# Two pooled PSUM buffers in place of one four-bank tile, in a fused long-convolution and gated feed-forward kernel

## The chip, the cores and the metric

The kernel runs on one core of a Trainium2 chip. The metric is the device time of one execution in microseconds, the median of several runs. Profiles are of one execution each, taken by the hardware profiler; their times count from the start of the span.

## What is computed

The input `x` (2048 tokens, 640 channels, bf16) is layer-normalised; a gated convolution and a gated feed-forward block of the normalised input are added to it:

```python
x = A_q
xn = _layernorm(x, axis=-1)
# A: k_shift = causal 4-tap filter of k, per channel;  kv = k_shift * v
#    y = irfft(rfft(kv, padded to 2S) * rfft(ssm_k, padded to 2S))[:S] + kv * ssm_D
#    result: xn * y
# B: (sigmoid(xn @ w_gate) * (xn @ w_up)) @ w_down      (640 -> 1728 -> 640)
return x + A(xn, k, v, ...) + B(xn, ...)
```

## The kernel before

Two streams of work share the engines. The **feed-forward** goes over four token tiles of 512 tokens. For each tile TensorE (PE) does 13 `gate` steps (L225) and 13 `up` steps (L233) of five 128x512 matmuls, one `both` step (L240) for the last half block, and 16 `down` steps (L252) of seven 128x320 matmuls, two to an output. ScalarE (ACT) applies the sigmoid (L231), VectorE (DVE) multiplies (L238) and adds the projection into `x` (L262). Four transposes `xn_tr` (L211) prepare the next tile. Their PSUM buffers come from a pool of four one-bank buffers, `psG`.

The **convolution** goes over five chunks of 128 channels. A transform of 2048 points is done as two matmul stages forward and two back, with trips through DRAM to rearrange the data between them. The steps of a chunk:

- `kv_op` (L289): the 4-tap filter times `v`, on DVE, in 16 operations; `h_tr` (L281), twice: eight PE transposes of the filter, then an ACT copy into `kvh` (L287).
- `st1` (L317), eight times: four 128x256 matmuls (L328), an ACT copy of 128x1024 to `t1` (L331). Each second one is written to DRAM (`wr1`).
- `rd2` reads it back rearranged, `st2` (L349), four times: sixteen 32x32 matmuls of 512 columns (L355) into all four banks, an ACT copy of 128x2048 (L357).
- `prod` (L362), a shuffle (L366) and a product (L368) on DVE.
- `inv1` (L371), twice: 64 small matmuls into all four banks (L383), an ACT copy of 128x2048 (L386); then `wr2` to DRAM and `rdb` back (one buffer `bi`).
- `inv2` (L402), twice: sixteen matmuls (L409); DVE multiplies by `xn` straight out of PSUM (L413) and adds into `x` (L414).

All of these use one PSUM tile, `pc`, four banks of 512 fp32 columns (L269). `st1`, `h_tr` and `inv2` take half of it by `two` (L272), which flips between banks 0-1 and banks 2-3; `st2` and `inv1`, the middle stages, use the whole. With `psG` this fills the eight banks.

The waits between engines are derived by the framework from which tiles an instruction touches; a pool hands out a buffer again when all users of the tile that last held it are done.

The order of all instructions is written by a planner inside the kernel (L449 on). It keeps estimates of when each engine is free and when each piece of data is ready, and takes in turn a step of the feed-forward sequence or, where its inputs and buffers would be ready, a step of the convolution's chains. For each step a list gives engine, duration, needs and products; `C` (L485) counts halves of `pc`, so that a step needs the half of two uses before, and a middle stage takes two. The planner's order fixes each engine's queue; SP's queue of DMA issues too.

Of the kernel before, what the change touches and what calls it, by code (L numbers as in the profile page):

```python
# [10 lines left out]
BF16 = mybir.dt.bfloat16  # L11
F32 = mybir.dt.float32
U16 = mybir.dt.uint16
ACT = mybir.ActivationFunctionType
ALU = mybir.AluOpType
# [4 lines left out]
P = 128  # L20
# [3 lines left out]
NQ = 4  # L24
# [33 lines left out]
def kernel(  # L58
# [14 lines left out]
    nc = tc.nc  # L73
# [14 lines left out]
    res = ctx.enter_context(tc.tile_pool(name="res", bufs=1))  # L88
    cv = ctx.enter_context(tc.tile_pool(name="cv", bufs=1))
    dr = ctx.enter_context(tc.tile_pool(name="dr", bufs=1, space=bass.MemoryType.DRAM))  # L90
    psC = ctx.enter_context(tc.tile_pool(name="psC", bufs=1, space=bass.MemoryType.PSUM))
    psG = ctx.enter_context(tc.tile_pool(name="psG", bufs=4, space=bass.MemoryType.PSUM))

    ident = res.tile([P, P], BF16, name="ident")
# [8 lines left out]
    SM = SMt.bitcast(BF16)  # L103

    x = res.tile([P, NB, DM], BF16, name="x")
    xn = res.tile([P, NB, DM], BF16, name="xn")
# [158 lines left out]
        sync.dma_start(outr[:, b, :], x[:, b, :])  # L265

    pc = psC.tile([P, 4, 512], F32, name="pc")  # L269
    turn = [0]  # L270

    def two(dtype):  # L272
        turn[0] ^= 1
        t = pc[:, 2 * turn[0]:2 * turn[0] + 2, :]
        return t if dtype == F32 else t.bitcast(dtype)

    def add_D(c):
        d = cin[c]
        nc.gpsimd.tensor_tensor(d["hn"][:, 0:1], d["hn"][:, 0:1], d["dcl"][:, :], ALU.add)

    def h_tr(c, part):  # L281
        d = cin[c]
        hv = d["hn"].rearrange("c (p b) -> c b p", b=NB)
        pt = two(BF16)[:, 0, :].rearrange("p (i c) -> p i c", i=8)
        for i in range(8):
            nc.tensor.transpose(pt[:, i, :], hv[:, 8 * part + i, :], ident[:])  # L286
        nc.scalar.copy(out=d["kvh"][:, 8 * part:8 * part + 8, 1, :], in_=pt)  # L287

    def kv_op(c, n):  # L289

# [23 lines left out]
    def quad(i):  # L314
        return slice(32 * i, 32 * i + 32)

    def st1(c, n):  # L317

        h, n4 = divmod(n, 4)
        d = chunks[c]  # L320
        if n == 0:
            d["d1"] = dr.tile([P, 2, NB, 2 * P], BF16, name="d1", bufs=2)
        if n % 2 == 0:
            d["t1"] = cv.tile([P, 8, 2, P], BF16, name="t1", bufs=2)
        ps = two(F32).rearrange("p k (i f) -> p (k i) f", i=2)
        for i in range(4):
            b = 4 * n4 + i
            nc.tensor.matmul(ps[:, i, :], lhsT=S1[:, b, h, :], rhs=cin[c]["kvh"][:, b, :, :],  # L328
                             start=True, stop=True)
        o = 4 * (n % 2)  # L330
        nc.scalar.copy(out=d["t1"][:, o:o + 4, :, :].rearrange("p b s c -> p b (s c)"), in_=ps)  # L331
        d[n // 2] = d["t1"]

    def wr1(c, k):
# [14 lines left out]
    def st2(s):  # L349

        d = groups[s]
        d["xz"] = cv.tile([P, 3, 8, P], BF16, name="xz", bufs=3)
        for g in range(4):
            for q in range(NQ):
                nc.tensor.matmul(pc[quad(g), q, :], lhsT=SM[quad(q), 0, :],  # L355
                                 rhs=d["t2"][quad(q), 2 * g:2 * g + 2, :], start=True, stop=True)
        nc.scalar.copy(out=d["xz"][:, 0:2, :, :].rearrange("p s (q e) c -> p q e s c", q=NQ),  # L357
                       in_=pc.rearrange("p q (e s c) -> p q e s c", e=2, s=2))

    swap = [(i + 16) % 32 for i in range(32)]  # L360

# [9 lines left out]
    def inv1(y):  # L371

        c, y2 = divmod(y, 2)
        d = chunks[c]
        if y2 == 0:
            d["d2"] = dr.tile([32, P, P], BF16, name="d2", bufs=2)
        ao = cv.tile([P, 16, P], BF16, name="ao")
        for o in range(2):
            xz = groups[2 * y + o]["xz"]
            for i in range(2):  # L380
                for q in range(NQ):
                    for g in range(4):
                        nc.tensor.matmul(pc[quad(q), g, 256 * o:256 * o + 256], lhsT=SM[quad(g), 1 + i, :],  # L383
                                         rhs=xz[quad(g), 1 + i, 2 * q:2 * q + 2, :],
                                         start=(i == 0), stop=(i == 1))
        nc.scalar.copy(out=ao.rearrange("p (s g e) c -> p g s (e c)", s=2, g=4),  # L386
                       in_=pc.rearrange("p g (s f) -> p g s f", s=2))
        d["ao"] = ao

    def wr2(y):  # L390
# [11 lines left out]
    def inv2(c, n):  # L402

        cs = slice(c * P, (c + 1) * P)
        ps = two(F32).rearrange("p k (i c) -> p (k i) c", c=P)
        for i in range(8):
            b = 8 * n + i
            for h in range(2):
                nc.tensor.matmul(ps[:, i, :], lhsT=TB[:, h, b, :], rhs=chunks[c]["bi"][:, h, i, :],  # L409
                                 start=(h == 0), stop=(h == 1))  # L410
        bs = slice(8 * n, 8 * n + 8)
        yx = cv.tile([P, 8, P], BF16, name="yx", tag="tmp")
        nc.vector.tensor_tensor(yx[:, :, :], ps, xn[:, bs, cs], ALU.mult)  # L413
        nc.vector.tensor_tensor(x[:, bs, cs], x[:, bs, cs], yx[:, :, :], ALU.add)  # L414


# [23 lines left out]
    xn_tr(0, 3, "dve")  # L440
    add_D(0)
    h_tr(0, 0)
    h_tr(0, 1)


# [39 lines left out]
    def C(i=0, back=2):  # L485
        k = count["C"] + i
        return ("C", k), (("C", k - back) if k >= back else None)
# [5 lines left out]
    def prior(tag, *k):  # L493
        return (tag,) + k if min(k) >= 0 else None

    def s_st1(c, n):
        def ops():
            mk, nd = C()
            n4 = n % 4
            k = 4 * c + n // 2  # L500
            o = [("PE", 0.45, [nd, "S1", ("kv", c, n4 // 2), ("h", c, n4 // 2)], [("st1", c, n)]),
                 ("ACT", 0.92, [("st1", c, n), prior("d1", k - 2)], [mk, ("t1", c, n)])]
            return o
        return st1, (c, n), ops
# [8 lines left out]
    def s_st2(s):  # L513
        def ops():
            m0, n0 = C()
            m1, n1 = C(1)
            return [("PE", 0.47, [n0, n1, ("t2", s), "SM"], [("st2", s)]),
                    ("ACT", 1.65, [("st2", s), prior("inv1", (s - 3) // 2) if s > 2 else None], [m0, m1, ("xh", s)])]
        return st2, (s,), ops

    def s_prod(s, n):
# [2 lines left out]
    def s_inv1(y):  # L524
        def ops():
            m0, n0 = C()
            m1, n1 = C(1)
            return [("PE", 0.75, [n0, n1, ("prod", 2 * y + 1)], [("inv1", y)]),
                    ("ACT", 1.65, [("inv1", y), prior("d2", y - 1)], [m0, m1, ("ao", y)])]
        return inv1, (y,), ops  # L530

    def s_rdb(c, n):
# [3 lines left out]
    def s_inv2(c, n):  # L536
        def ops():
            mk, nd = C()
            return [("PE", 0.95, [nd, ("bi", c, n), ("xn", 2 * n + 1, 3), "TB"], [("inv2", c, n)]),
                    ("DVE", 1.15, [("inv2", c, n)], [mk, ("yx", c, n)]),  # L540
                    ("DVE", 0.62, [("yx", c, n)], [("xa", c, n)])]
        return inv2, (c, n), ops

    def s_htr(c, part):
        def ops():
            mk, nd = C()
            return [("PE", 0.55, [nd, ("D", c), ("va", c)], [("htr", c, part)]),
                    ("ACT", 0.92, [("htr", c, part), prior("st1", c - 2, 7)], [mk, ("h", c, part)])]
        return h_tr, (c, part), ops
# [217 lines left out]
```

## Time and profile before

| | us |
|---|---|
| median of 3 runs | 287.39 (286.69 to 287.74) |
| the profiled execution | 286.87 |
| its span, first to last instruction | 285.1 |
| PE busy | 240.5 (84%) |
| DVE busy | 181.2 (64%) |
| ACT busy | 151.0 (53%) |
| POOL busy | 29.1 (10%) |
| DMA, share of 16 engines' time, queue 1 | 64.2% |

The PE figure counts matmuls with modelled ends; neighbouring matmuls overlap, so start-to-start distances tell more than lengths. The mean granted TensorE clock was 0.999. By time of start, the four token tiles' feed-forward parts begin at about 15, 76, 152 and 228 us; the first `st1` starts at 26.26, the last `inv2` at 273.56.

### The profile page before, as it was taken

How to read it: one execution, taken by the hardware profiler on the slowest of the kernel's cores; microseconds unless marked ns; L12 is line 12 of the kernel's file. 1: busy time of each engine (PE TensorE's matmuls, PEld its weight loads, DVE VectorE, ACT ScalarE, POOL GpSimd, SP SyncE). 2: the span in 40 equal slices, each digit the busy share in tenths (PEclk: the TensorE clock that was granted, in tenths of full speed). 3: DMA queues.
4: the chain of work that ended last, by engine and by line, in shares of the span. 5: the costliest groups of instructions: out<-in, count | busy, mean ns of one | idle time of the engine just before them, and what ended most of it. 6: DMA issues, size and time to landing. Idle time of an engine off the chain costs nothing. (4 is left out here: it accounts for less than half of the span.)

```text
span 285.1 us, 5834 instructions
## 1 busy us (share of the span) xinstructions
PE 240.5 (84%) x2428; PEld 138.4 (49%) x2428; DVE 181.2 (64%) x312; ACT 151.0 (53%) x156; POOL 29.1 (10%) x40
## 2 busy tenths in 40 slices
PE   0498988998888888897888788888878999999994
PEld 0444444566544433465564344443556644544773
DVE  3539959498788969889675455241564647683461
ACT  2733365146777667643677555666623977445000
POOL 4300108110010338010000000000000000000000
PEclk9999999999999999999999999999999999999999
DMA  6999798988878786861967430564642547502274
GB/s 198 246 356 368 186 302 247 264 202 200 256 243 236 199 242 232 258 228 39 245 180 240 155 143 2 181 190 148 222 149 76 183 111 226 147 2 77 74 281 163
DMA packets 84310, 54.84 MB, mean 192 GB/s; under 512 B 46844, under 2 KB 77372, under 8 KB 84028
## 3 DMA queue, kind: packets, MB, share of 16 engines
q1 hardware_dynamic: 83996, 53.95, 64.2%
q10 hardware_dynamic: 288, 0.52, 0.6%
q8 instruction: 19, 0.31, 0.5%
q14 instruction: 7, 0.06, 0.1%
HBM read 36.12 MB, written 18.35 MB: 191 GB/s over the span
## 5 line engine op out<-in xcount | busy, mean ns | idle before, releaser
L238 DVE TENSOR_TENSOR hT<-sig,pu 128x512 bf16<-128x512 bf16 x52 | 35.6, 684 | 57.9 <-PE pu L236 46.4
L228 PE MATMUL pg<-xnT,w 128*128 128x512 bf16 x260 | 65.8, 385 | 0.0
L259 PE MATMUL pd<-wd,hT 128*128 128x320 bf16 x448 | 65.4, 300 | 0.0
L236 PE MATMUL pu<-xnT,w 128*128 128x512 bf16 x260 | 65.2, 382 | 0.0
L331 ACT CAST t<-pc 128x1024 bf16<-128x1024 f32 x40 | 40.5, 1011 | 33.4 <-PE pc L328 27.6
L231 ACT ACTIVATE sig<-pg 128x512 bf16<-128x512 f32 x52 | 31.1, 598 | 38.9 <-PE pg L228 37.1
L259 PEld LDWEIGHTS <-hT 128*128 128x128 bf16 x448 | 42.6, 98 | 17.3 <-issue 1.4
L328 PE MATMUL pc<-kvh,S1t 128*128 128x256 bf16 x160 | 23.9, 272 | 26.0 <-ACT t L331 14.9
L357 ACT CAST xz<-pc 128x2048 bf16<-128x2048 f32 x20 | 37.3, 1863 | 14.3 <-PE pc L355 14.2
L228 PEld LDWEIGHTS <-w 128*128 128x128 bf16 x260 | 24.9, 99 | 28.4 <-issue 2.2
L236 PEld LDWEIGHTS <-w 128*128 128x128 bf16 x260 | 24.4, 98 | 28.2 <-issue 2.7
L328 PEld LDWEIGHTS <-S1t 128*128 128x128 bf16 x160 | 15.4, 97 | 35.1 <-issue 30.1
L262 DVE TENSOR_TENSOR x<-pd,x 128x320 bf16<-128x320 f32 x32 | 15.6, 488 | 23.1 <-PE pd L259 23.0
L368 DVE TENSOR_TENSOR xz<-xz 128x2048 bf16<-128x2048 bf16 x20 | 24.6, 1232 | 0.6
L307 DVE TENSOR_TENSOR acc<-acc,tmp 128x1024 bf16<-128x1024 bf16 x30 | 22.5, 748 | 1.0
L386 ACT CAST ao<-pc 128x2048 bf16<-128x2048 f32 x10 | 18.7, 1865 | 5.0 <-PE pc L383 4.9
L305 DVE TENSOR_TENSOR tmp<-kx,sc 128x1024 bf16<-128x1024 bf16 x30 | 20.6, 688 | 0.2
L187 DVE BATCH_NORM_STATS2 st<-x 128x6 f32<-128x320 bf16 x32 | 13.9, 475 | 4.6 <-DMA x<-in_A_q_dram 4.6
L287 ACT COPY kvh<-pc 128x1024 bf16<-128x1024 bf16 x10 | 10.1, 1013 | 10.7 <-PE pc L286 10.6
L215 PE MATMUL pt<-ident,xn 128*128 128x128 bf16 x80 | 7.7, 242 | 9.6 <-ACT xn L204 9.6
L413 DVE TENSOR_TENSOR yx<-pc,xn 128x1024 bf16<-128x1024 f32 x10 | 12.2, 1218 | 5.0 <-PE pc L409 5.0
L366 DVE STREAM_SHUFFLE xz<-xz 128x512 f32<-128x512 f32 x20 | 14.4, 722 | 0.0
(40 smaller groups left out, 149.9 us busy)
## 6 DMA issues: line engine op xcount, KB each, us to landing
d<-t SPq DMA_DIRECT2D x20, 512.0 KB, 3.1
t<-d SPq DMA_DIRECT2D x20, 512.0 KB, 4.8
d<-ao SPq DMA_DIRECT2D x10, 512.0 KB, 4.0
bi<-d SPq DMA_DIRECT2D x10, 512.0 KB, 4.5
out_dram<-x SPq DMA_DIRECT2D x16, 160.0 KB, 2.2
kx<-in_A_k_dram SPq DMA_DIRECT2D x16, 128.0 KB, 3.5
kvh<-in_A_v_dram SPq DMA_DIRECT2D x16, 128.0 KB, 3.5
hn<-in_A_ssm_k_dram SPq DMA_DIRECT2D x8, 256.0 KB, 4.9
```

The lines of the kernel that those rows point to most:

```text
L228: nc.tensor.matmul(pg[:, :], lhsT=w[:, c, fc * P:(fc + 1) * P], rhs=xnT[:, c, :], start=(c == 0), stop=(c == NC - 1))
L231: nc.scalar.activation(sig[fc][:, :], pg[:, :], ACT.Sigmoid)
L236: nc.tensor.matmul(pu[:, :], lhsT=w[:, c, UP + fc * P:UP + (fc + 1) * P], rhs=xnT[:, c, :], start=(c == 0), stop=(c == NC - 1))
L238: nc.vector.tensor_tensor(hT[:, fc, :], sig[fc][:, :], pu[:, :], ALU.mult)
L259: nc.tensor.matmul(pd[:, :], lhsT=hT[:, fc, bb * P:(bb + 1) * P], rhs=wd[:, fc, es], start=(fc == 0), stop=(fc == NFC - 1))
L305: nc.vector.tensor_tensor(d["tmp"][:, :, :], kx[:, lo + 3 - m:hi + 3 - m, :], sb(m), ALU.mult)
L307: nc.vector.tensor_tensor(d["acc"][:, :, :], d["acc"][:, :, :], d["tmp"][:, :, :], ALU.add)
L328: nc.tensor.matmul(ps[:, i, :], lhsT=S1[:, b, h, :], rhs=cin[c]["kvh"][:, b, :, :], start=True, stop=True)
L331: nc.scalar.copy(out=d["t1"][:, o:o + 4, :, :].rearrange("p b s c -> p b (s c)"), in_=ps)
L357: nc.scalar.copy(out=d["xz"][:, 0:2, :, :].rearrange("p s (q e) c -> p q e s c", q=NQ), in_=pc.rearrange("p q (e s c) -> p q e s c", e=2, ...
L368: nc.vector.tensor_tensor(xz[:, 1:3, :, :], xz[:, 0:1, :, :].to_broadcast((P, 2, 8, P)), xz[:, 1:3, :, :], ALU.mult)
L386: nc.scalar.copy(out=ao.rearrange("p (s g e) c -> p g s (e c)", s=2, g=4), in_=pc.rearrange("p g (s f) -> p g s f", s=2))
```

## The change

The tile `pc` and the helper `two` go. The pool `psC` gets two buffers, and each step takes tiles of two banks from it under one tag; `st2` and `inv1` take two tiles, send their matmuls to one or the other by bank, and evict with two ACT copies of 128x1024 instead of one of 128x2048. In the planner's lists the middle stages' ACT entry of 1.65 becomes two of 0.92, the first of which gives one half back. The planner's order changes with its estimates; the number of PE steps of each kind stays the same.

```diff
-    psC = ctx.enter_context(tc.tile_pool(name="psC", bufs=1, space=bass.MemoryType.PSUM))
+    psC = ctx.enter_context(tc.tile_pool(name="psC", bufs=2, space=bass.MemoryType.PSUM))
...
-    pc = psC.tile([P, 4, 512], F32, name="pc")
-    turn = [0]
-
-    def two(dtype):
-        turn[0] ^= 1
-        t = pc[:, 2 * turn[0]:2 * turn[0] + 2, :]
-        return t if dtype == F32 else t.bitcast(dtype)
...
     def h_tr(c, part):
-        pt = two(BF16)[:, 0, :].rearrange("p (i c) -> p i c", i=8)
+        pt = psC.tile([P, 8, P], BF16, name="pht", tag="c")
...
     def st1(c, n):
-        ps = two(F32).rearrange("p k (i f) -> p (k i) f", i=2)
+        ps = psC.tile([P, 4, 2 * P], F32, name="ps1", tag="c")
...
     def st2(s):
+        ps = [psC.tile([P, 2, 2, 2, P], F32, name="ps2", tag="c") for _ in range(2)]
         for g in range(4):
             for q in range(NQ):
-                nc.tensor.matmul(pc[quad(g), q, :], lhsT=SM[quad(q), 0, :],
+                nc.tensor.matmul(ps[q // 2][quad(g), q % 2, :, :, :], lhsT=SM[quad(q), 0, :],
                                  rhs=d["t2"][quad(q), 2 * g:2 * g + 2, :], start=True, stop=True)
-        nc.scalar.copy(out=d["xz"][:, 0:2, :, :].rearrange("p s (q e) c -> p q e s c", q=NQ),
-                       in_=pc.rearrange("p q (e s c) -> p q e s c", e=2, s=2))
+        for n in range(2):
+            nc.scalar.copy(out=d["xz"][:, 0:2, 4 * n:4 * n + 4, :].rearrange("p s k c -> p k s c"),
+                           in_=ps[n].rearrange("p q e s c -> p (q e) s c"))
...
     def inv1(y):
+        ps = [psC.tile([P, 2, 512], F32, name="psa", tag="c") for _ in range(2)]
...
-                        nc.tensor.matmul(pc[quad(q), g, 256 * o:256 * o + 256], lhsT=SM[quad(g), 1 + i, :],
+                        nc.tensor.matmul(ps[g // 2][quad(q), g % 2, 256 * o:256 * o + 256], lhsT=SM[quad(g), 1 + i, :],
...
-        nc.scalar.copy(out=ao.rearrange("p (s g e) c -> p g s (e c)", s=2, g=4),
-                       in_=pc.rearrange("p g (s f) -> p g s f", s=2))
+        dst = ao.rearrange("p (s g e) c -> p g s (e c)", s=2, g=4)
+        for n in range(2):
+            nc.scalar.copy(out=dst[:, 2 * n:2 * n + 2, :, :],
+                           in_=ps[n].rearrange("p g (s f) -> p g s f", s=2))
...
     def inv2(c, n):
-        ps = two(F32).rearrange("p k (i c) -> p (k i) c", c=P)
+        ps = psC.tile([P, 8, P], F32, name="psb", tag="c")
...
     def s_st2(s):
-                    ("ACT", 1.65, [("st2", s), prior("inv1", (s - 3) // 2) if s > 2 else None], [m0, m1, ("xh", s)])]
+                    ("ACT", 0.92, [("st2", s), prior("inv1", (s - 3) // 2) if s > 2 else None], [m0]),
+                    ("ACT", 0.92, [("st2", s)], [m1, ("xh", s)])]
...
     def s_inv1(y):
-                    ("ACT", 1.65, [("inv1", y), prior("d2", y - 1)], [m0, m1, ("ao", y)])]
+                    ("ACT", 0.92, [("inv1", y), prior("d2", y - 1)], [m0]),
+                    ("ACT", 0.92, [("inv1", y)], [m1, ("ao", y)])]
```

More of the change, by code (lines that the diff above doesn't have):

```diff
@@ L283, in h_tr @@
         hv = d["hn"].rearrange("c (p b) -> c b p", b=NB)
-        pt = two(BF16)[:, 0, :].rearrange("p (i c) -> p i c", i=8)
+        pt = psC.tile([P, 8, P], BF16, name="pht", tag="c")
         for i in range(8):
             nc.tensor.transpose(pt[:, i, :], hv[:, 8 * part + i, :], ident[:])
-        nc.scalar.copy(out=d["kvh"][:, 8 * part:8 * part + 8, 1, :], in_=pt)
+        nc.scalar.copy(out=d["kvh"][:, 8 * part:8 * part + 8, 1, :], in_=pt[:, :, :])
     def kv_op(c, n):
@@ L330, in st1 @@
         o = 4 * (n % 2)
-        nc.scalar.copy(out=d["t1"][:, o:o + 4, :, :].rearrange("p b s c -> p b (s c)"), in_=ps)
+        nc.scalar.copy(out=d["t1"][:, o:o + 4, :, :].rearrange("p b s c -> p b (s c)"), in_=ps[:, :, :])
         d[n // 2] = d["t1"]
@@ L412, in inv2 @@
         yx = cv.tile([P, 8, P], BF16, name="yx", tag="tmp")
-        nc.vector.tensor_tensor(yx[:, :, :], ps, xn[:, bs, cs], ALU.mult)
+        nc.vector.tensor_tensor(yx[:, :, :], ps[:, :, :], xn[:, bs, cs], ALU.mult)
         nc.vector.tensor_tensor(x[:, bs, cs], x[:, bs, cs], yx[:, :, :], ALU.add)
```

## The prediction

> **What bounds the kernel now.** I first read the page's busy shares: PE 240.5 us of a 285.1 us span, DVE 181.2, ACT 151.0, with the TensorE clock granted in full throughout. PE runs in order and is rarely far from busy, so the end is set by PE's own work plus the places where it stands still. The view of who waited for whom, cut to PE, lists these (us in total, times, longest):
>
> ```profile
> PE pc L328 <- ACT t L331: 14.9, 13, 1.3
> ...
> PE pc L328 <- DVE yx L413: 8.6, 5, 1.8
> PE pc L286 <- ACT kvh L287: 2.3, 2, 1.2
> PE pc L328 <- ACT kvh L287: 2.2, 2, 1.1
> PE pc L286 <- ACT t L331: 2.2, 2, 1.1
> ```
>
> Apart from 9.6 us at the start (the line left out, waiting for normalised input) nearly all of PE's waiting is for evictions out of `pc`. The timeline shows which eviction (start, length, engine, line, then the idle time before it):
>
> ```profile
> 85.56 0.60 PE L328 MATMUL pc<-kvh,S1t 128*128 128x256 bf16 x4
> ...
> 86.19 1.01 ACT L331 CAST t<-pc 128x1024 bf16<-128x1024 f32 x1 [0.26 <-PE pc L328]
> ...
> 87.26 0.60 PE L328 MATMUL pc<-kvh,S1t 128*128 128x256 bf16 x4 [1.10 <-ACT t L331]
> 87.69 1.24 PE L228 MATMUL pg<-xnT,w 128*128 128x512 bf16 x5
> ```
>
> Two first-stage steps stand next to each other and take turns on the halves of `pc`. The second writes the half that is free, yet it starts at 87.26, just after the copy out of the *other* half ends (86.19 + 1.01 = 87.20). So the two halves do not work as two buffers: each writer waits for the last reader of the tile as a whole. The same after the last inverse stage, whose half VectorE empties:
>
> ```profile
> 161.12 1.06 PE L409 MATMUL pc<-bi,TBt 128*128 128x128 bf16 x16
> ...
> 162.75 1.21 DVE L413 TENSOR_TENSOR yx<-pc,xn 128x1024 bf16<-128x1024 f32 x1
> ...
> 164.01 0.60 PE L328 MATMUL pc<-kvh,S1t 128*128 128x256 bf16 x4 [1.83 <-DVE yx L413]
> ```
>
> 162.75 + 1.21 = 163.96, and L328 goes at 164.01, again into the half that nobody was reading.
>
> **What the change takes away.** Two tiles from a pool are two separate things to wait for. The order of the changed program's instructions shows it: of 13 first-stage steps that directly follow another, two wait for no eviction, and eleven wait for the eviction of the step that last held their own buffer, none for that of the step just before. So the waits above go, and I price them: 14.9 + 8.6 + 2.3 + 2.2 + 2.2 = 30.2 us, and a single one of 0.3 before L409 makes 30.5. The idle column is short of the loss: a step shown as 0.60 lets the next start 0.43 later where nothing holds it (87.26 to 87.69), so a held pair, 1.70 from start to start, loses 1.27 and not 1.10. 0.17 more for each of 25 waits is 4.2. Five more steps, with one feed-forward step of 1.08 (or a projection step of 0.96) between them and the step before, start 0.18 to 0.30 late by their start times (38.37, 40.06, 95.93, 142.38, 188.19): 1.0. Sum: 30.5 + 4.2 + 1.0 = 35.7. PE's own work is the same: 278 steps, 2428 matmuls. With nothing in their place the span would be 285.1 - 35.7 = 249.4.
>
> The Trainium skill speaks against this. Perfetto Trace Analysis, Matmuls, wants matmul groups to rotate through different PSUM banks so that the eviction of one overlaps the next; the halves already do. By that rule alone the change would free nothing (time near 287). The trace differs, with 1.10 us of idle in front of the other half.
>
> **What it adds.** Each of 30 middle evictions becomes two copies of half the size:
>
> ```profile
> L331 ACT CAST t<-pc 128x1024 bf16<-128x1024 f32 x40 | 40.5, 1011 | 33.4 <-PE pc L328 27.6 <-DVE x L414 4.3 <-ACT t L331 0.7
> ...
> L357 ACT CAST xz<-pc 128x2048 bf16<-128x2048 f32 x20 | 37.3, 1863 | 14.3 <-PE pc L355 14.2
> ```
>
> Last columns: busy us and mean ns of one, then idle before and its causes. A half copy is not in the trace; L331 moves as many elements of the same types, so I take 1.01. Two make 2.02, 0.16 over 1.86; 30 x 0.16 = 4.8 us of ACT. The bounds for one half are 0.93 (half of 1.86) and 1.86 (no saving). The Trainium skill (Perfetto Trace Analysis, Optimizing Scalar/DVE Operations) also speaks for fewer, larger copies: about 51 ns of overhead per ScalarE instruction on PSUM, twice that in profiled latency. An estimate from it is 30 x 0.10 = 3 us; the rows here give 0.16 a piece, and the forecast would be the same by either.
>
> What hides these 4.8 is PE. The tightest repeating stretch is a pair of L328 steps, gate and up, one middle step, gate and up. Today a round takes 6.92 (78.64 to 85.56, starts of two pairs). Unheld, PE needs 2 x 0.43 + 2.16 + 0.46 + 2.16 = 5.65; ACT needs 2 x 1.01 + 2 x 0.60 + 2.02 = 5.24. From the start of a pair: its copies end at 1.64 and 2.65; PE reaches the middle step, which takes both buffers, at 3.03, so no wait. The sigmoid fits in until 3.25, the half copies run from 3.58 (0.55 after the matmuls start, as at 83.02 to 83.57) to 4.59 and 5.60, and the next pair wants its buffers at 5.65 and 6.08. It holds, by 0.38 at the least; without that cover up to 4.8 comes back. I put 0.5 on the path.
>
> **What is late next.** Four terms come back onto the 249.4.
> (a) Middle steps that follow L409 by two PE steps need its buffer 0.89 + 2.16 = 3.05 later; VectorE freed it 2.84 later above, with one shuffle (0.72) ahead of it. With a product (L368, 1.23) ahead as well it is about 1.0 late. About four such places, and queued behind PE's wait is the feed-forward work: 0 to 4, I take 2.
> (b) VectorE. The windows view (length; PE, PEld, DVE, ACT, POOL busy; clock; DMA share):
>
> ```profile
> 0.00:76.50 76.50, 60.14 (x460) 35.21 (x461) 53.49 (x104) 35.42 (x43) 14.38 (x25) 1.00 0.93 258
> 76.50:152.00 75.50, 64.02 (x704) 37.25 (x699) 63.40 (x113) 48.88 (x48) 14.69 (x15) 1.00 0.71 213
> ```
>
> DVE has 116.9 us of work up to 152, the end of the second token tile. Adding the losses above by their times, 21.8 of the 35.7 us lie there (8.4 of them before 76.5), so PE could be done at 130. The new order moves some DVE work out of the second tile's feed-forward part (counts times mean durations: 43.7 before, 38.7 after) into the third's (21.0, 29.3), which leaves some 112 to that point, and 10.8 us in which DVE waits for the input (4.6) and the first gate and up (6.2). 123 against 130 is cover on average, but in the second tile 38.7 of DVE stand against 39.5 of PE, and what DVE delivers late (kv products, `hT`) holds PE. 0 to 5, I take 2.5.
> (c) DMA. In the first 76.5 us the queues hold 0.93 x 76.5 = 71.1 us of work; with 8.4 freed there PE would want the same in 68.1. 3.0 too much, some of it prefetch that can slide. SP issues the same transfers in a slightly different order: the first store of L386 now stands ahead of a load of the filter and of `x`, and the inverse table's load stands behind the loads of `v` of a chunk; what is pushed back is wanted a tile's part later. 0 to 3, I take 1.5.
> (d) The half copies: 0 to 4.8, taken as 0.5.
> Together 6.5, with ends 0 and 16.8. The end of the kernel keeps its form: the last two L409 still have four projection steps between them against a read that took 3.94, and five instead of seven steps follow, which leaves PE's last matmul as the last piece.
>
> **Sum.** 249.4 + 6.5 = 255.9 of span. The profiled execution took 286.87 for 285.1 of span, 1.8 more: 257.7. The median of the runs, 287.39, stands 0.5 above that execution: 258.2.
>
> **Rivals.**
> 1. *DVE and DMA bind the first half.* For it: 38.7 against 39.5, and DMA at 0.93. Against it: DVE waits 46.4 us for L236 today, so it is mostly early. If half of the 21.8 fails to come, 258.2 + 10.9 - 2.5 = 266.6; if none does, 277.5.
> 2. *The change does not separate the buffers.* The waits stay, and the longer evictions add up to 4.8: 287 to 292. The waits in the changed program's order speak against it.
> 3. *Slower: the half copies cost as much as whole ones.* Place: the rounds above. ACT then needs 2 x 1.01 + 1.20 + 2 x h; it passes PE's 5.65 at h = 1.22, and today's 6.92 at h = 1.85. At h = 1.9, 30 x 1.94 = 58 us more ACT, and rounds of 7.02: about 0.1 over today in some 20 middle rounds, 2 us, so 289 to 290. Against it: 512, 1024 and 2048 columns take 0.60, 1.01 and 1.86, which is a fixed 0.16 and a price per column.
>
> **How the numbers follow.** Forecast (252 to 268): 0.85. Rival 1 (beyond 268, still faster): 0.10. Rival 2: 0.02, half of it within 0.5%. Rival 3: 0.03. I predict 258.2. The low end 252 is all of the 35.7 with nothing returned (249.4 + 1.8 + 0.5 = 251.7); the high end 269 is all four terms at their upper ends (268.5). The range leaves out most of rival 1 and the other two. Half a per cent, 1.4 us, is about what a measurement of this kernel can tell from no change: faster 0.95, same 0.01, slower 0.04.
>
> **What would show it.** Right: no idle before the second of two adjacent first-stage steps, start to start 0.43; the PE waits on evictions down from 30 us to under 5; two copies near 1.01 in place of 1.86; rounds near 5.7. Wrong in size: new PE waits for the kv product, for the transforms' reads, or for L409's eviction above 10 us; DVE over 95% busy in the second tile. Wrong in kind: waits of 1.1 in front of the second of a pair.

## The result and the profile after

| | before | after |
|---|---|---|
| median of the runs, us | 287.04 (4 runs, 286.58 to 287.74) | 254.11 (4 runs, 252.25 to 255.56) |
| span of the profiled execution | 285.1 | 252.9 |
| PE busy | 240.5 (84%) | 235.4 (93%) |
| ACT busy | 151.0 | 150.0 |
| DVE busy | 181.2 | 179.0 |

The ratio is 0.885, with a 95% interval of 0.878 to 0.891: 33 us less. Two executions in the experiments, of 622.28 us in the fifth and of 271.82 us in the seventh, stand apart from the others of their kernel for a reason that no run shows, and the times given below leave them out. PE's waits in the changed kernel, all that the view lists (us in total, times, longest):

```profile
PE pt L215 <- ACT xn L204: 9.5, 3, 8.3
PE psb L405 <- DMA bi<-d: 1.9, 4, 1.0
PE pg L244 <- ACT sig L231: 0.7, 1, 0.7
PE pht L277 <- DMA hn<-in_A_ssm_k_dram: 0.6, 1, 0.6
PE psb L405 <- DMA TBt<-tabTB: 0.4, 1, 0.4
PE ps L347 <- DMA t<-d: 0.3, 1, 0.3
```

Not one wait on the eviction of a convolution buffer is left, where there were 30.5 us. The first line is the start of the kernel, as before. The line numbers have moved: L319 is the first stage's matmul now (L328 before), L322 its copy, L347 and L350 those of `st2`, L377 and L382 those of `inv1`, L405 and L409 those of `inv2`.

The timeline of PE in the second token tile, which shows the rounds that the prediction worked out (start, length, line, matmuls):

```profile
68.94 1.04 PE L319 MATMUL ps<-kvh,S1t 128*128 128x256 bf16 x8
69.81 1.24 PE L228 MATMUL pg<-xnT,w 128*128 128x512 bf16 x5
70.89 1.24 PE L236 MATMUL pu<-xnT,w 128*128 128x512 bf16 x5
72.07 0.43 PE L347 MATMUL ps<-t,SMt 32*32 32x512 bf16 x16
72.43 1.25 PE L228 MATMUL pg<-xnT,w 128*128 128x512 bf16 x5
73.52 1.24 PE L236 MATMUL pu<-xnT,w 128*128 128x512 bf16 x5
74.60 1.04 PE L319 MATMUL ps<-kvh,S1t 128*128 128x256 bf16 x8
```

Two first-stage steps are now so close that the view merges them into one piece of eight matmuls, and the next step starts 0.87 after it. A round takes 74.60 - 68.94 = 5.66 us. Before it took 6.92, from the step below to the one at 85.56 that the prediction shows:

```profile
78.64 0.60 PE L328 MATMUL pc<-kvh,S1t 128*128 128x256 bf16 x4
```

ACT, in the page's groups, first the changed kernel's and then the one group of before that the prediction does not show:

```profile
L350 ACT CAST xz<-ps 128x1024 bf16<-128x1024 f32 x40 | 38.5, 1017 | 12.0 <-PE ps L347 11.7
L322 ACT CAST t<-ps 128x1024 bf16<-128x1024 f32 x40 | 39.1, 1018 | 9.6 <-PE ps L319 5.4
...
L382 ACT CAST ao<-psa 128x1024 bf16<-128x1024 f32 x20 | 19.3, 1017 | 8.1 <-PE psa L377 4.5
```

```profile
L386 ACT CAST ao<-pc 128x2048 bf16<-128x2048 f32 x10 | 18.7, 1865 | 5.0 <-PE pc L383 4.9
```

A half copy takes 1.017, but 40 of them are 38.5 us busy and not 40.7, since the second of a pair starts before the first has ended. For 20 middle evictions of `st2` that is 38.5 against 37.3 us before, for ten of `inv1` 19.3 against 18.7.

### The profile page after: what moved, and what is told of

It is laid out like the page before. It is cut to its first block, busy times and chain, and to the rows that moved or that the text cites. A ratio compares the mean times of both kernels' runs of the same rounds, so it can differ in the third digit from the quotient of the medians.

```text
span 252.9 us, 5862 instructions
## 1 busy us (share of the span) xinstructions
PE 235.4 (93%) x2428; PEld 138.3 (55%) x2428; DVE 179.0 (71%) x312; ACT 150.0 (59%) x186; POOL 27.8 (11%) x40
## 4 chain that ended last, share of the span: by engine, by line
PE 69%; DMA 23%; DVE 2%; ACT 2%; SPq 1%; issue 1%; ACTq 0%
PE pg L228 17%; PE pu L236 17%; PE pd L259 17%; DMA bi<-d 9%; DMA d<-t 6%; PE ps L319 5%; PE psb L405 4%; DMA TBt<-tabTB 3%; PE psa L377 3%; PE ps L347 3%; DMA t<-d 2%; DMA x<-in_A_q_dram 2%; PE pht L277 2%; PE pt L215 2%; DMA d<-ao 2%; DVE st L187 1%
## 5 line engine op out<-in xcount | busy, mean ns | idle before, releaser
L228 PE MATMUL pg<-xnT,w 128*128 128x512 bf16 x260 | 64.8, 380 | 0.0
L238 DVE TENSOR_TENSOR hT<-sig,pu 128x512 bf16<-128x512 bf16 x52 | 35.3, 681 | 35.7 <-PE pu L236 25.8
L350 ACT CAST xz<-ps 128x1024 bf16<-128x1024 f32 x40 | 38.5, 1017 | 12.0 <-PE ps L347 11.7
L322 ACT CAST t<-ps 128x1024 bf16<-128x1024 f32 x40 | 39.1, 1018 | 9.6 <-PE ps L319 5.4
L382 ACT CAST ao<-psa 128x1024 bf16<-128x1024 f32 x20 | 19.3, 1017 | 8.1 <-PE psa L377 4.5
L298 DVE TENSOR_TENSOR acc<-acc,tmp 128x1024 bf16<-128x1024 bf16 x30 | 21.9, 729 | 1.0
L319 PE MATMUL ps<-kvh,S1t 128*128 128x256 bf16 x160 | 21.9, 273 | 0.0
L319 PEld LDWEIGHTS <-S1t 128*128 128x128 bf16 x160 | 15.4, 98 | 5.8 <-issue 0.3
L409 DVE TENSOR_TENSOR yx<-psb,xn 128x1024 bf16<-128x1024 f32 x10 | 12.2, 1220 | 6.2 <-PE psb L405 6.1
L278 ACT COPY kvh<-pht 128x1024 bf16<-128x1024 bf16 x10 | 10.1, 1017 | 8.2 <-PE pht L277 8.1
```

The costliest lines, as they stand in the source:

```text
L228: nc.tensor.matmul(pg[:, :], lhsT=w[:, c, fc * P:(fc + 1) * P], rhs=xnT[:, c, :], start=(c == 0), stop=(c == NC - 1))
L238: nc.vector.tensor_tensor(hT[:, fc, :], sig[fc][:, :], pu[:, :], ALU.mult)
L298: nc.vector.tensor_tensor(d["acc"][:, :, :], d["acc"][:, :, :], d["tmp"][:, :, :], ALU.add)
L350: nc.scalar.copy(out=d["xz"][:, 0:2, 4 * n:4 * n + 4, :].rearrange("p s k c -> p k s c"), in_=ps[n].rearrange("p q e s c -> p (q e) s c"))
L382: nc.scalar.copy(out=dst[:, 2 * n:2 * n + 2, :, :], in_=ps[n].rearrange("p g (s f) -> p g s f", s=2))
```

## The experiments

Each was compared with the kernel before on the same chip (287.4 to 287.5 us there).

**1. Two tiles, old order.** Is it the separation of the buffers, or the new order of the planner? The diff is against the changed kernel; `h_tr`, `st1` and `inv2` take their half by `two` again, and the middle stages take both tiles.

```diff
-    psC = ctx.enter_context(tc.tile_pool(name="psC", bufs=2, space=bass.MemoryType.PSUM))
+    psC = ctx.enter_context(tc.tile_pool(name="psC", bufs=1, space=bass.MemoryType.PSUM))
...
+    pcs = [psC.tile([P, 2, 512], F32, name="pc%d" % i) for i in range(2)]
+    turn = [0]
+
+    def two(dtype):
+        turn[0] ^= 1
+        t = pcs[turn[0]][:, :, :]
+        return t if dtype == F32 else t.bitcast(dtype)
...
+                    ("ACT", 1.65, [("st2", s), prior("inv1", (s - 3) // 2) if s > 2 else None], [m0, m1, ("xh", s)])]
...
+                    ("ACT", 1.65, [("inv1", y), prior("d2", y - 1)], [m0, m1, ("ao", y)])]
```

> Two tiles of two banks, allocated once, in place of pc; the middle stages evict with two copies; the planner keeps the old lists, so the order of PE's steps is that of the kernel before. Theory (the gain is the wait on the whole tile): nearly all of it comes with the old order, 253 to 259 us, and no PE wait on the eviction of the step just before. Rival (the new lists and the new order bring a large part): 262 to 275 us.

Measured: 254.44 us, ratio 0.886 (0.882 to 0.890). Its PE waits behind the start:

```profile
PE pc L385 <- DVE xz L369: 1.3, 1, 1.3
PE pc L285 <- DMA hn<-in_A_ssm_k_dram: 1.2, 1, 1.2
PE pc L355 <- DVE yx L417: 0.6, 1, 0.6
PE pc L413 <- DMA bi<-d: 0.5, 2, 0.3
```

Of the waits on evictions 0.6 us is left here (L355 for VectorE's read at L417), and the interval covers the changed kernel's ratio of 0.885. Neither the pool nor the planner's new lists are needed for the gain; two separate tiles are.

**2. The split alone.**

```diff
-        nc.scalar.copy(out=d["xz"][:, 0:2, :, :].rearrange("p s (q e) c -> p q e s c", q=NQ),
-                       in_=pc.rearrange("p q (e s c) -> p q e s c", e=2, s=2))
+        for n in range(2):
+            nc.scalar.copy(out=d["xz"][:, 0:2, 4 * n:4 * n + 4, :].rearrange("p s (q e) c -> p q e s c", q=2),
+                           in_=pc[:, 2 * n:2 * n + 2, :].rearrange("p q (e s c) -> p q e s c", e=2, s=2))
...
```

`inv1` likewise, with the tile and the planner as before.

> One tile pc as before, old lists; only the middle evictions are split into two copies of half the size. Theory: the wait on the whole tile stays, so 286 to 290 us, with PE idle before L328 near 26 us. Rival (a half given back early is what pays): 275 us or less.

Measured: 287.57 us, ratio 1.0015 (0.9996 to 1.0034). The waits of the kernel before stand there almost to the tenth:

```profile
PE pc L328 <- ACT t L331: 14.8, 13, 1.3
...
PE pc L328 <- DVE yx L416: 8.8, 5, 1.9
```

On the one tile, where PE waits anyway, the split costs nothing that can be measured, and it gains nothing by itself.

**3. The order alone.** The kernel before, with the planner's two lists changed as in the diff and nothing else.

> One tile pc and one copy as before; only the planner's lists are the new ones (two entries of 0.92 for a middle eviction), which gives the new order of steps. Theory: the order by itself brings nothing, 283 to 292 us. Rival (the order matters): 275 us or less.

Measured: 289.44 us, ratio 1.008 (1.006 to 1.011): the new order on the old tile is 2 us worse, and PE still waits 14.7 us for the copies of L331. Its waits add up to no more than before; in the profile one of them is longer, and slow matmuls follow it (a gate or an up usually takes 1.24):

```profile
167.75 0.95 PE L328 MATMUL pc<-kvh,S1t 128*128 128x256 bf16 x4 [2.68 <-DVE yx L413]
168.49 2.34 PE L228 MATMUL pg<-xnT,w 128*128 128x512 bf16 x5
170.62 1.56 PE L236 MATMUL pu<-xnT,w 128*128 128x512 bf16 x5
```

By start times that costs 1.7 us, most of the 2.

**4. Plain slices.** Does the reshaped view hide which banks a step uses?

```diff
-        ps = two(F32).rearrange("p k (i f) -> p (k i) f", i=2)
+        turn[0] ^= 1
+        k0 = 2 * turn[0]
...
-            nc.tensor.matmul(ps[:, i, :], lhsT=S1[:, b, h, :], rhs=cin[c]["kvh"][:, b, :, :],
+            nc.tensor.matmul(pc[:, k0 + i // 2, 256 * (i % 2):256 * (i % 2) + 256], lhsT=S1[:, b, h, :], rhs=cin[c]["kvh"][:, b, :, :],
...
```

> One tile pc as before; only the first stage names its half by plain slices of pc, without the helper two and without reshaping. Theory (any use of one tile waits for the last reader of the whole tile): 1.1 us idle before the second of two adjacent first-stage steps stays, about 287 us. Rival (the reshaped view hides which banks are used): that idle goes for first-stage pairs, 268 us or less.

Measured: 286.74 us in one run. The timeline of PE, with the first stage's matmuls at L329 in this kernel:

```profile
85.31 0.60 PE L329 MATMUL pc<-kvh,S1t 128*128 128x256 bf16 x4
87.01 0.60 PE L329 MATMUL pc<-kvh,S1t 128*128 128x256 bf16 x4 [1.10 <-ACT t L332]
87.44 1.24 PE L228 MATMUL pg<-xnT,w 128*128 128x512 bf16 x5
```

The 1.10 is still there, with the half named by a plain index. Together with experiment 1: what a step waits for is the tile.

**5. ACT's cover.** An engine's cover is the time by which it can be late before PE has to wait. The changed kernel, in which the second half copy of each middle stage is done once more.

```diff
-        for n in range(2):
+        for n in (0, 1, 1):
```

> The changed kernel with the second of the two half copies of every middle stage done once more: 30 x 1.01 = 30 us more for ACT (and 0.9 later for what follows). Theory (the 4.8 us that the split costs are hidden because ACT has room): the 30 us are mostly hidden too, as a round then needs 6.25 of ACT against 5.65 of PE in some 15 of the rounds: 258 to 266 us. Rival (ACT is already on the path): 275 us or more.

Measured: 270.99 us (267.07 to 271.03), ratio 0.937 (0.932 to 0.943), 13 to 17 us over the changed kernel's 254.11. That is above the 258 to 266 expected and below the rival's 275. The same kernel once more:

> The kernel with the third half copy again, for a profile of an undisturbed execution: 267 to 271 us; in it the time over the changed kernel, 13 to 17 us, should stand as PE waiting for half copies of the middle stages (theory: the buffer that is copied twice is late for the next step), or else for the shuffle and product on VectorE that follow (rival).

Measured: 268.39 us, span 266.6. PE's waits in it:

```profile
PE ps L319 <- ACT xz L350: 3.4, 7, 0.7
PE psb L405 <- DMA bi<-d: 2.7, 4, 1.9
PE ps L319 <- ACT ao L382: 1.8, 4, 0.8
PE pht L277 <- POOL hn L270: 1.5, 1, 1.5
...
PE ps L347 <- ACT xz L350: 0.5, 1, 0.5
PE psa L377 <- DVE xz L361: 0.5, 1, 0.5
...
```

Some 7 us of waits for half copies of the middle stages are new (3.4 + 1.8 + 0.5 and smaller ones), by start times 9.7 of the 13.7 us that this execution is longer. VectorE's shuffle and product account for 0.5. So the buffers are late first, as the theory had it. The cover that hides the split's own cost (1.8 us more in the two groups above, not the 4.8 forecast) is real, but it ends soon: ACT is busy 28.3 us more here, and about half of that shows.

**6. VectorE's cover.** The changed kernel with ten more operations on DVE.

```diff
+            for _ in range(2):
-            nc.vector.tensor_tensor(d["acc"][:, :, :], kx[:, lo + 3:hi + 3, :], sb(0), ALU.mult)
+                nc.vector.tensor_tensor(d["acc"][:, :, :], kx[:, lo + 3:hi + 3, :], sb(0), ALU.mult)
```

> The changed kernel with the first tap product of the filter done twice, ten operations of 0.69 us more on VectorE, all in the first 160 us. Theory (VectorE has cover, which the prediction priced at a loss of 2.5): 0 to 2 us more than the changed kernel, 254 to 256. Rival (VectorE sets the pace of the second tile): 259 us or more.

Measured: 258.0 us, ratio 0.896 (0.895 to 0.898): 3.9 over the changed kernel for 6.9 us of work, between the theory (up to 256) and the rival (from 259). In its profile matmuls wait for DVE, which none does in the changed kernel:

```profile
PE ps L348 <- DVE yx L410: 1.6, 1, 1.6
PE psa L378 <- DVE xz L362: 1.1, 1, 1.1
```

An estimate from this is about 3 us of cover in the first 160 us (6.9 - 3.9). VectorE does not bind, but little is left.

**7. DMA.** The changed kernel with each first-stage store issued twice, first to the same place, then to a scratch tile of its own.

```diff
         sync.dma_start(d["d1"][:, h, 8 * part:8 * part + 8, :], d[k].rearrange("p b s c -> p b (s c)"))
+        more = dr.tile([P, 8, 2 * P], BF16, name="more", bufs=8)
+        sync.dma_start(more[:, :, :], d[k].rearrange("p b s c -> p b (s c)"))
```

To the same place:

> The changed kernel with every store of the first stage issued twice, 20 x 512 KB more, the same bytes to the same place. Theory (a DMA share near 1.0 in the first 126 us is a bound): 12 of the stores lie there, 6.3 MB at about 275 GB/s, so 10 to 20 us more, 264 to 275. Rival (the share counts transfers that overlap, and what is late is prefetch): 259 us or less.

Measured: 304.79 us, ratio 1.060 (1.056 to 1.064), worse than either theory. SP's waits show why it is no measure of the DMA itself:

```profile
SPq L329 <- DMA d<-t: 81.4, 20, 6.8
```

The second store waited on SP for the first to land, 4.1 us each time, with every other issue queued behind it. To a place of its own:

> The changed kernel with a second store of every first-stage tile into a scratch place of its own, so that it waits for no earlier store of the same bytes: 20 x 512 KB more DMA, no added wait on the first store's landing. Theory (the 50 us that storing twice to one place cost were SP standing behind the first store, 81 us in its waits; DMA itself is close to full in the first 126 us): 10 to 20 us over the changed kernel, 264 to 275. Rival (the share near 1.0 does not bound): 254 to 259 us. Third (DMA is the bound and 50 us was its price): 290 us or more.

Measured: 268.31 us (266.89 to 269.15), 13 to 15 us more for 10.5 MB, inside the theory's range. The DMA queues are close to a bound in the changed kernel's first half: their share, 1.02 up to 68 us and 0.94 from there to 126, only rises to 1.02 and 1.01. One way this reaches PE is by ACT, in whose queue the copies into `t1` wait for the earlier stores and hold up the sigmoids behind them. First the line of ACT's waits, then those of PE's:

```profile
ACT t L322 <- DMA more<-t: 9.9, 5, 6.6
```

```profile
PE pg L244 <- ACT sig L231: 3.4, 1, 3.4
PE ps L349 <- DMA t<-d: 2.6, 1, 2.6
```

But the time is not all waiting for transfers. PE's timeline behind the longest wait:

```profile
48.74 2.29 PE L244 MATMUL pg<-xnT,w 128*128 128x512 bf16 x5 [3.43 <-ACT sig L231]
50.83 6.74 PE L259 MATMUL pd<-wd,hT 128*128 128x320 bf16 x35
```

In the changed kernel the same two pieces take 1.24 and 4.92. The granted clock was 0.50 from 48.7 to 52 us, and again behind the wait of 2.6. By start times, matched step by step, the profiled execution is 12.0 us longer than the changed kernel's: some 4.7 are PE's waits for ACT, some 3 its waits for transfers, and some 4 are these slow matmuls. The 13 to 15 us are thus more than the price of the transfers alone. The store to the same place was hit by this too: its mean granted clock was 0.941.

**8. The start alone.** The kernel before, with the filter's transposes of the first chunk in buffers of `psG`.

```diff
-        pt = two(BF16)[:, 0, :].rearrange("p (i c) -> p i c", i=8)
+        if c == 0:
+            pg = psG.tile([P, 8, P], BF16, name="ph0", tag="g")
+            pt = pg[:, :, :]
+        else:
+            pt = two(BF16)[:, 0, :].rearrange("p (i c) -> p i c", i=8)
```

> The kernel before with the filter transposes of the first chunk alone in buffers of psG; everything later waits as before. Theory (in the changed kernel the first gates also ran at full speed 1.3 us sooner, because the idle of 1.1 us between the two transposes was gone): 1.6 + 1.3 us less than before, 284 to 285.2. Rival (only the idle goes, or the first weights set the start): 285.5 to 287.4.

Measured: 285.15 us, ratio 0.992 (0.990 to 0.993): 2.4 us less. That is more than the 1.3 us that the held pair of transposes loses by start times; where the rest comes from is taken up in the last section.

## Why the prediction came out

254.11 against 258.2: inside the range, and the mechanism was the one forecast. Point by point.

*What the waits were.* Right. Experiment 1 gives the whole gain with two tiles and the old order; experiments 2, 3 and 4 leave the tile and lose it. The reading that decided was the distance between two start times: the second step began 0.06 after the end of a copy out of the half it did not use. The Trainium skill's rule on rotating banks (Perfetto Trace Analysis, Matmuls) was kept by the kernel before as well; in these runs rotating banks was not enough as long as they were parts of one tile.

*The 35.7 us.* Right as far as the profiles show. The floor it gave, 249.4 of span, is 3.5 under the 252.9 measured. By start times about 4.8 came back, and the start gave 1.3 that was not priced: the first gate and up lost 1.5 us to slow matmuls before and 0.2 in the profile after. 249.4 + 4.8 - 1.3 = 252.9. The 1.3 may be luck of the executions profiled (see the last section).

*What comes back, 6.5.* Too much, and made up of the wrong terms. The waits that returned are 1.9 + 0.7 + 0.6 + 0.4 + 0.3 = 3.9 of idle, of which 0.2 was there before, or the 4.8 by start times. All of them are for transfers, one by way of ACT. By term:

- (a) late evictions of the last inverse stage (L409 then, L405 now) by VectorE, taken as 2: none. No step waits for it in the changed kernel. In experiment 1, with the old order, it is 0.6.
- (b) VectorE, taken as 2.5: no matmul waited for it (weight loads of L377 did, 0.7 us). The prediction set 38.7 us of VectorE's work against 39.5 of PE's in the second tile. The durations of its instructions do add up to 37.5 there, but neighbours overlap in the trace, so that it was busy only 34.6 of 39.0 us. Experiment 6 puts its cover at 3 us. In experiment 1 VectorE was busy 56.1 of the 58 us between 68 and 126, and matmuls waited 1.3 for its product.
- (c) DMA, taken as 1.5 with 3 as the upper end: too little. 3.2 of idle stand in the view as waits for transfers, and mostly not where the prediction put them: 0.6 + 0.4 + 0.3 in the first half, and the 1.9 for `bi` in the second. Those reads have one buffer: on SP their issue waited 10.6 us for the read before to land, 6.3 for the stores they read and 4.5 for L405 to be done with the buffer. No run tried two. The 0.7 of L244 belongs here as well, though the view names a sigmoid. That sigmoid stood on ACT behind two copies into `t1`, which had waited 3.8 us for an earlier store:

```profile
43.77 1.93 ACT L322 CAST t<-ps 128x1024 bf16<-128x1024 f32 x2 [3.81 <-DMA d<-t]
45.58 1.11 ACT L231 ACTIVATE sig<-pg 128x512 bf16<-128x512 f32 x2
```

- (d) the half copies, taken as 0.5: none. No middle stage had run when L244 waited, at 46.25; the first starts at 55.73. Two copies take 1.93 from start to end and not 2.02, ACT's busy time did not rise, and experiment 2 shows the split at no cost.

So the terms that failed in size are (a) and (b), which were too large, and (c), which was too small. In (b) I priced a resource at 98% of a stretch, by adding up whole durations, and as if some of it had to come through. That the sum comes within 2 us of what returned is luck.

*The distance of 4.1 us* between 258.2 and 254.11 is then 1.3 from the start, 1.7 from terms that were too large together, and 1.2 because the median lay 0.7 under the profiled execution and not 0.5 above it, up to rounding.

*The rivals.* DVE and DMA in the first half: windows of the changed kernel (length; PE, PEld, DVE, ACT, POOL busy; clock; DMA share; GB/s) show how near it was. The last is the second tile's gates and ups.

```profile
0.00:68.00 68.00, 56.90 (x453) 34.30 (x454) 52.69 (x102) 35.17 (x46) 14.61 (x25) 1.00 1.02 280
68.00:126.00 58.00, 57.62 (x645) 33.17 (x643) 51.76 (x101) 44.30 (x54) 12.99 (x14) 1.00 0.94 268
69.81:108.84 39.03, 39.03 (x406) 19.79 (x403) 34.59 (x70) 32.63 (x41) 11.21 (x12) 1.00 0.94 270
```

PE is busy throughout the second stretch with DMA at 0.94, DVE at 89% and ACT at 76%. Buffers that were not separated: experiment 4 is what that rival looks like, and it is not the changed kernel. Half copies as dear as whole ones: 1.017 against 1.86.

## What to carry to other kernels

Two halves of one tile are two buffers only if what orders the engines treats them as two. Look in the timeline at whether the writer of the free half starts with the end of the copy from the other half; if so, allocate two tiles and split what spans both. Before counting on the whole of such a gain, add up each other engine and the DMA share over the shortened stretch, by the time that an engine is busy and not by the sum of its durations. Here all of them just fitted, and 7 us more of VectorE, 30 more of ACT or 10 MB more of DMA each took 4 to 17 us back.

## What the hardware showed that was not expected

**Half-speed matmuls at the start.** The first gate's matmuls run at half speed, 0.43 us each and not 0.22, while the profile gives the granted clock of that time as 1.00. The timeline before, and then that of experiment 1, which has no idle between the transposes:

```profile
14.24 1.01 PE L286 MATMUL pc<-ident,hn 128*128 128x128 bf16 x8 [1.10 <-ACT kvh L287]
15.05 2.34 PE L228 MATMUL pg<-xnT,w 128*128 128x512 bf16 x5
```

```profile
11.73 1.91 PE L285 MATMUL pc<-ident,hn 128*128 128x128 bf16 x16
13.43 2.34 PE L228 MATMUL pg<-xnT,w 128*128 128x512 bf16 x5
15.57 1.40 PE L236 MATMUL pu<-xnT,w 128*128 128x512 bf16 x5
```

In the profile of the changed kernel the same gate took 1.39. In the kernel before, full speed came 3.8 us after its last idle; in the changed kernel about 3.1 us after PE's work became unbroken, in experiment 1 5.2. The Trainium skill (TensorE: Matmul & The Clock Gate, What's actually happening) describes half rate until one window of about 3.4 us has been busy, with a window that runs freely. The spread here agrees with that: in the seven profiles without the idle between the transposes, the first gate and up lost 0 to 1.3 us to it, and in the four with it 1.1 to 1.5. That the 1.1 us of idle caused the slow gates, as experiment 8 supposed, is therefore not shown. In its profile the transposes gave 1.3 us and faster first gates 1.4, and the second is a size that also varies by luck.

**Half speed after a wait.** Behind the start, and leaving out the execution of 622.28 us, PE waited 123 times between 1.0 and 2.1 us in the profiles of this case, and no half-speed matmul followed. It waited ten times for 2.6 us or more, once in experiment 3 and nine times in the two kernels of experiment 7, and half-speed matmuls followed each time. The granted clock does show these: 0.50 behind both long waits of the second kernel of experiment 7. No wait between 2.1 and 2.6 us was measured.

**Two copies in a row on ACT** overlap: 1.93 from the start of the first to the end of the second, where 2 x 1.017 are 2.03:

```profile
78.26 1.93 ACT L350 CAST xz<-ps 128x1024 bf16<-128x1024 f32 x2 [0.59 <-PE ps L347]
```

The 0.10 agrees with the 93 ns that the Trainium skill gives (ScalarE: Activation LUTs, What ACT_TABLE_LOAD costs).

**A DMA share of 1.02 over 68 us** held PE up by 1.6 us of idle (0.7 + 0.6 + 0.3), though the median landing of a first-stage store rose from 3.1 to 4.1 us and that of a transform's read from 4.8 to 5.7 (medians over the whole kernel).
